# Operand sums and three of the chunk sums on GpSimd instead of VectorE, in a gated scan with two feed-forward layers

## The chip, the core and the metric

The kernel runs on one core of a Trainium2 chip. The metric is device microseconds of one execution. In the profile PE is TensorE's matmuls, PEld its weight loads, DVE is VectorE, ACT is ScalarE, POOL is GpSimd and SP the engine that issues DMAs.

## What is computed

Three stages on 6080 tokens of 256 features, all in float32: a gated scan along the tokens, a feed-forward layer with a leaky ReLU, a second one with an ELU.

```
sig = 1 / (1 + exp(-f_logit));  f = lower_bound + (1 - lower_bound) * sig
h[t] = f[t] * h[t-1] + (1 - f[t]) * x[t]                 # the scan, 256 features
y1 = max(0.01 * a, a) @ w_out1,      a = h  @ w_in1      # 256 -> 2048 -> 256
y2 = elu(b) @ w_out2,                b = y1 @ w_in2      # 256 -> 2048 -> 256
```

## The kernel before

**Tiling.** Tokens go in 12 chunks: 11 of 512 and one of 448 (the fifth). Features lie on the 128 partitions, tokens along the free axis. The 2048 inner features are taken in 4 groups (q = 0 to 3) of 512. For every layer, chunk and group there is an in-projection, the activation, and an out-projection that adds into the chunk's output banks. A chunk of a layer takes PE about 40 us.

**Precision.** Each float32 operand is split in a high part (a cast to fp32r, by ScalarE) and a low part (value less high part, by VectorE), and each product is made of three matmuls (lines 611, 612, 613).

**Seven products instead of eight.** The in-projection of a chunk (from the third chunk of layer 1 on, and in all of layer 2) is done as a 2 x 2 block product with seven block products and some sums (Strassen's way, in Winograd's form). The sums of the weights are made once. The sums of the data are made for each chunk in operands(): four subtractions of 128 x 256, T1 to T4, on the tile bt (the helper comb, line 455). T2 needs T1, T4 needs T2. Then split() casts the blocks to their high parts on ScalarE (L459) and makes their low parts on VectorE (L461), in three pieces: the plain blocks B11, B22, B21; then T1, T2, T3; then T4. The splits are held back until the group before the chunk's first has begun (hold). The tile bt exists once: its next filling, by two scans (L579) in layer 1, by two DMAs from y1d (L599) in layer 2, begins when the last split is done.

**Inside a group** the seven products run into two banks and one seed bank. Products feed each other through snapshots: ScalarE copies a bank (L658, L694), VectorE adds bank and snapshot (L661, one input in PSUM), and the next products go into the banks that these leave free. The activations are L707, L712 (layer 1) and L717 to L734 (layer 2); the gated values are split for the out-projection by L750 and L753.

**Two groups of four** have their odd half of the out-projection done with seven products too (seven(); chunks 4 to 12 of layer 1 with q = 1, 2, and chunks 1 to 11 of layer 2 with q = 0, 1). Their operands are summed in odd_operands() (L842) and split there (L854, L857). They leave two further banks, "s" and "z", which leave() folds into the chunk's two output banks: ScalarE copies both into an SBUF tile of four quarters (L903); u2 (L905) adds quarter 1 to quarter 2; u4 (L906) adds that to quarter 0; L907 adds quarters 0 and 1 to output bank 1; "both" (L910, 128 x 512, its second input one quarter read twice) makes a partial sum in SBUF; L915 adds output bank 0 to it. In layer 1 the result goes to y1d by DMA; in layer 2 it is transposed (L929) and stored.

**Banks.** There are 7 PSUM banks and one seed bank, handed out from a pool in the planned order.

**The order of the work.** Nothing is issued as it stands in the code. Each step is handed to a planner (class Plan, emit) as an operation of an engine with a cost formula (v1, v2 for VectorE, s1 for ScalarE, mm for PE), the operations it comes after, the tiles it takes and gives back, and a due time that is carried backwards through the operations that use it. The planner starts, engine by engine, the operation that can start first, and among those that can start within 0.1 us the one that is due first. The order that comes out is fixed in each engine's queue, and each engine works its queue in order. Before the change GpSimd has one kind of planned operation, sg (L368, in weights()): 32 instructions of one input, 128 x 512, which help to rebuild the weights' float32 values. The last 16 of them are spread over 165 to 406 us.

Of the kernel before, what the change touches and what calls it, by code (L numbers as in the profile page):

```python
# [15 lines left out]
ALU = mybir.AluOpType  # L16
# [96 lines left out]
def kernel(  # L113
# [24 lines left out]
    nc = tc.nc  # L138
# [69 lines left out]
    def v1(n):  # L208
        return 0.07 + n / 960.0
# [3 lines left out]

    def s1(n):
        return 0.09 + n / 1200.0

    def mm(n):
        return (n * 0.000451 + 0.0025 if n < CH else 0.2272) if n != HC else 0.1136
# [6 lines left out]
    def dve(*a, **k):  # L225
        return plan.add("DVE", *a, **k)

    def act(*a, **k):
        return plan.add("ACT", *a, **k)

    def pool(*a, **k):
        return plan.add("POOL", *a, **k)

    def dma(*a, **k):
        return plan.add("SP", *a, **k)

    def free(after, give):

        plan.add("-", 0.0, 1e6, lambda: None, after, give=give)
# [18 lines left out]
    for l, c, q in stream:  # L258
        n = sizes[c]
# [52 lines left out]
    def weights(l, u, due, gate=()):  # L312
# [45 lines left out]
        def val():  # L358
# [10 lines left out]
            out=fr(), in0=top().bitcast(I8), scalar1=2.0, scalar2=-2.0, op0=ALU.min, op1=ALU.max,  # L369
        ), [ld], take=[(b, "wf", "ws")])  # L370
        ex = act(s1(n) + 0.1, None, lambda: nc.scalar.activation(
            out=sc().bitcast(I32), in_=tile_("up"), func=AF.Relu, scale=2.0**27, bias=gbias,
        ), [up, sg], give=[(b, "up", "up")])
# [64 lines left out]
    def operands(c, filled, take, read=(), hold=()):  # L438


        n = sizes[c]
        h = n // 2
        xb = {"done": {}}
        bt = take

        def f32(s, e=None):
            return bt["bt"][2].bitcast(F32)[:, s * h : (e or s + 1) * h]

        def part(j, s, e):

            name, s, e = ("pb", s - 1, e - 1) if 1 <= s < 4 else ("pt", s and s - 3, (s and e - 3) or 1)
            return xb[name][2][:, 4 * HC * j + s * h : 4 * HC * j + e * h]

        def comb(o, i, j, after):
            return dve(v1(h), None, lambda: nc.vector.tensor_tensor(
                out=f32(o), in0=f32(i), in1=f32(j), op=ALU.subtract), after)

        def split(s, e, after, last):
            hi = act(s1((e - s) * h), None, lambda: nc.scalar.copy(out=part(0, s, e), in_=f32(s, e)), after,  # L459
                     take=[(xb, "pb" if s == 1 else "pt", "op")] if s else [])  # L460
            lo = dve(v1((e - s) * h), None, lambda: nc.vector.tensor_tensor(  # L461
                out=part(1, s, e), in0=f32(s, e), in1=part(0, s, e).bitcast(F32), op=ALU.subtract,
            ), [hi], give=[(bt, "bt", bt["pool"])] if last else [])
            for i in range(s, e):
                xb["done"][i] = [lo]
            return hi, lo

        t1 = comb(T1, B12, B11, filled[:1])
        t3 = comb(T3, B22, B12, filled)
        t2 = comb(T2, B22, T1, [t1] + filled[1:])  # L470
        t4 = comb(T4, B21, T2, [t2, t1, t3])
        one = split(1, 4, [*filled, *hold], False)
        two = split(4, 7, [t1, t2, t3, one[0], *hold], False)
        split(0, 1, [t4, two[0], one[1], two[1], *read], True)

        def op(s):
            return tuple(part(j, s, s + 1) for j in (0, 1))

        xb["op"] = op
        return xb  # L480

    def rows(c, filled, take, read=()):
# [26 lines left out]
        out=fa, in0=lb, scalar1=-0.5, scalar2=0.5, op0=ALU.mult, op1=ALU.add), [ab])  # L509
    ab = dve(0.07, None, lambda: nc.vector.tensor_scalar(  # L510
        out=fb, in0=lb, scalar1=0.5, scalar2=0.5, op0=ALU.mult, op1=ALU.add), [ab])
# [353 lines left out]
    def leave(l, c, i, yb, swapped):  # L865
        n, t0 = sizes[c], starts[c]
        if swapped:
            for t in range(n // P):
                ob = {}

                def move(t=t, ob=ob):
                    dst, ps = ob["o"][2][:, :D], yb[t // 2][2][:, t % 2 * D : (t % 2 + 1) * D]
                    if t // 2:
                        nc.vector.tensor_copy(out=dst, in_=ps)
                    else:
                        nc.scalar.copy(out=dst, in_=ps)

                def send(t=t, ob=ob):
                    nc.sync.dma_start(out=out[t0 + t * P : t0 + (t + 1) * P, :], in_=ob["o"][2][:, :D])

                ev = (dve if t // 2 else act)(v1(D), due_in[i] + 20.0, move, [yb["touched"][t // 2]],
                                              take=[(ob, "o", "raw" if t % 2 else "t")],
                                              give=[(yb, t // 2, "bank")] if t % 2 else [])
                dma(DMA, due_in[i] + 20.0, send, [ev], give=[(ob, "o", "raw" if t % 2 else "t")], late=LATE)
            return
        h = n // 2
        soon = due_in[i] + 26.0
        last = yb["touched"]
        ob = {k: {} for k in range(KD)}
        pool_ = "t" if l == 1 else "raw"  # L890

        def o(k):
            return ob[k]["o"][2][:, :n]

        done = {}
        if "s" in last:

            sb = {}

            def at(s, e=None):  # L900
                return sb["sb"][2][:, s * h : (e or s + 1) * h]

            cps = [act(s1(n), soon, lambda s=s, k=k: nc.scalar.copy(out=at(s, s + 2), in_=yb[k][2][:, :n]), [last[k]],  # L903
                       take=[(sb, "sb", "h")] if s == 0 else [], give=[(yb, k, "bank")]) for s, k in ((0, "s"), (2, "z"))]
            u2 = dve(v1(h), soon, lambda: nc.vector.tensor_tensor(out=at(2), in0=at(2), in1=at(1), op=ALU.add), cps)  # L905
            u4 = dve(v1(h), soon, lambda: nc.vector.tensor_tensor(out=at(0), in0=at(0), in1=at(2), op=ALU.add), [u2])  # L906
            done[1] = dve(v1(n), soon, lambda: nc.vector.tensor_tensor(  # L907
                out=o(1), in0=yb[1][2][:, :n], in1=at(0, 2), op=ALU.add), [u4, last[1]],
                take=[(ob[1], "o", pool_)], give=[(yb, 1, "bank")])
            both = dve(v1(n), soon, lambda: nc.vector.tensor_tensor(  # L910
                out=o(0).rearrange("p (a h) -> p a h", a=2),
                in0=at(0, 4).rearrange("p (a b h) -> p a b h", a=2, b=2)[:, :, 0, :],
                in1=at(3).unsqueeze(1).to_broadcast([P, 2, h]), op=ALU.add), [u4], take=[(ob[0], "o", pool_)])
            free([done[1], both], [(sb, "sb", "h")])
            done[0] = dve(v1(n), soon, lambda: nc.vector.tensor_tensor(  # L915
                out=o(0), in0=o(0), in1=yb[0][2][:, :n], op=ALU.add), [both, last[0]], give=[(yb, 0, "bank")])
        elif l == 1:
            for k in range(KD):
                done[k] = (act if k else dve)((s1 if k else v1)(n), None, lambda k=k: (
                    nc.scalar.copy if k else nc.vector.tensor_copy)(out=o(k), in_=yb[k][2][:, :n]),  # L920
                    [last[k]], take=[(ob[k], "o", pool_)], give=[(yb, k, "bank")])
        if l == 1:
            yd[c] = [dma(DMA, due_in[i] + 30.0, lambda k=k: nc.sync.dma_start(
                out=y1d[c][k * P : (k + 1) * P, :], in_=o(k)), [done[k]], give=[(ob[k], "o", pool_)], late=LATE)
                for k in (1, 0)]
            return
        for k in (1, 0):
            tb = {}
            tr = dve(v1(n), None, lambda tb=tb, k=k: nc.vector.transpose(  # L929
                out=tb["o"][2][:, :n], in_=o(k) if done else yb[k][2][:, :n]), [done.get(k), last[k]], take=[(tb, "o", "t")],  # L930
                give=[(ob[k], "o", pool_) if done else (yb, k, "bank")])
            sent = []
            for z in range(4):
                def send(tb=tb, k=k, z=z):
                    c0 = k * P + z * 32
                    nc.sync.dma_start(
                        out=out[t0 : t0 + n, c0 : c0 + 32].rearrange("(b i) j -> i b j", i=32),
                        in_=tb["o"][2][z * 32 : (z + 1) * 32, :n].rearrange("p (b j) -> p b j", j=32),
                    )

                sent.append(dma(DMA, due_in[i] + 40.0, send, [tr] + sent[-1:], give=[(tb, "o", "t")] if z == 3 else [],
                                late=LATE if z == 3 else 0.0))
# [19 lines left out]
    for i, (l, c, q) in enumerate(stream):  # L962
# [18 lines left out]
        at = len(prods)  # L981
# [40 lines left out]
```

## Time and profile before

| | |
|---|---|
| median of 3 runs | 998.78 us (998.7 to 1000.65) |
| span of the profiled execution | 999.4 us, 20315 instructions |
| PE busy | 986.1 us (99%) |
| PEld busy | 974.7 us (98%) |
| VectorE busy | 877.2 us (88%), 1352 instructions |
| ScalarE busy | 773.7 us (77%), 1135 instructions |
| GpSimd busy | 32.1 us (3%), 38 instructions |

The page gives no time of the profiled execution besides its span, the time from the first to the last instruction; the runs shown are executions of their own. A busy share is an average over the whole span. Neighbouring instructions of one engine overlap by some 0.08 us in the records, so that a group's busy time is a little more than the time that its engine spends on it.

### The profile page before, as it was taken

Reading aid. Unit: us, or ns where it says so; the run is one execution under the profiler, and the core shown is the slowest. Engines: PE = TensorE matmul, PEld = TensorE weight load, DVE = VectorE, ACT = ScalarE, POOL = GpSimd, SP = SyncE. Lnnn points to the kernel's source line nnn. Section 1 sums busy time; section 2 is a strip of 40 time slices with the busy share of each in tenths; the row PEclk is TensorE's granted clock in tenths of the full one; section 3 lists DMA queues with packets and bytes.
Section 4 is the critical chain, followed back from the end, with each engine's and each line's share of the span. In section 5 each row is a group of like instructions: output and inputs, shape, how many; then the busy total and the mean of one; then the engine's idle time right before and its main releaser. Section 6 shows DMA issues by size and latency. Waiting matters only on the chain.

```text
span 999.4 us, 20315 instructions
## 1 busy us (share of the span) xinstructions
PE 986.1 (99%) x8338; PEld 974.7 (98%) x8338; DVE 877.2 (88%) x1352; ACT 773.7 (77%) x1135; POOL 32.1 (3%) x38
## 2 busy tenths in 40 slices
PE   7999999999999999999999999999999999999998
PEld 6999999999999999999999999999999999999997
DVE  6899978999999999986678998988989989889875
ACT  5776687878978878777678787877887888788864
POOL 1111000010000000100000000000000000000000
PEclk9999999999999999999999999999999999999999
DMA  6533304155353553411760101101111021010110
GB/s 189 137 96 75 81 11 95 56 146 130 122 158 105 130 135 98 107 33 53 274 253 22 22 22 40 23 22 22 30 34 22 23 44 22 22 23 22 33 22 22
DMA packets 159086, 74.38 MB, mean 74 GB/s; under 512 B 132496, under 2 KB 146832, under 8 KB 158992
## 3 DMA queue, kind: packets, MB, share of 16 engines
q1 hardware_dynamic: 158992, 73.08, 27.1%
q8 instruction: 65, 1.06, 0.4%
q14 instruction: 29, 0.24, 0.1%
HBM read 48.01 MB, written 25.03 MB: 73 GB/s over the span
## 4 chain that ended last, share of the span: by engine, by line
PE 97%; DVE 1%; DMA 1%; ACT 0%; SPq 0%; issue 0%; DVEq 0%
PE bank L611 29%; PE bank L613 29%; PE bank L612 29%; PE seed L613 2%; PE seed L612 2%; PE seed L611 2%; DMA raw<-in_f_logit_dram 1%; PE bank L799 1%; PE bank L797 0%; PE bank L798 0%; DVE op L753 0%; PE bank L543 0%; DVE ws L378 0%; DVE ws L723 0%; DVE bt L579 0%
## 5 line engine op out<-in xcount | busy, mean ns | idle before, releaser
L613 PE MATMUL bank<-op,wI 128*128 128x256 f32 (+1 forms) x1152 | 319.3, 277 | 0.8 <-DVE wI L392 0.8
L611 PE MATMUL bank<-op,wI 128*128 128x256 f32 (+1 forms) x1152 | 320.0, 278 | 0.0
L612 PE MATMUL bank<-op,wI 128*128 128x256 f32 (+1 forms) x1152 | 319.1, 277 | 0.0
L611 PEld LDWEIGHTS bank<-op,wI 128*128 128x128 f32 x1152 | 217.4, 189 | 1.9 <-ACT sn L658 0.2
L612 PEld LDWEIGHTS bank<-op,wI 128*128 128x128 f32 x1152 | 217.3, 189 | 1.5 <-DVE op L498 0.2
L613 PEld LDWEIGHTS bank<-op,wI 128*128 128x128 f32 x1152 | 217.4, 189 | 1.2 <-DVE wI L392 1.2
L611 PE MATMUL bank<-op,wE 128*128 128x256 f32 (+2 forms) x662 | 191.1, 289 | 0.0
L612 PE MATMUL bank<-op,wE 128*128 128x256 f32 (+2 forms) x662 | 191.0, 288 | 0.0
L612 PE MATMUL bank<-op,wO 128*128 128x256 f32 (+2 forms) x680 | 189.4, 279 | 1.5 <-DVE op L753 1.5
L613 PE MATMUL bank<-op,wE 128*128 128x256 f32 (+2 forms) x662 | 190.8, 288 | 0.0
L611 PE MATMUL bank<-op,wO 128*128 128x256 f32 (+2 forms) x680 | 189.4, 278 | 0.0
L613 PE MATMUL bank<-op,wO 128*128 128x256 f32 (+2 forms) x680 | 189.2, 278 | 0.0
L661 DVE TENSOR_TENSOR h<-bank,sn 128x512 f32<-128x512 f32 (+1 forms) x176 | 119.5, 679 | 39.0 <-PE bank L613 30.0
L612 PEld LDWEIGHTS bank<-op,wO 128*128 128x128 f32 x680 | 127.8, 188 | 1.8 <-DVE op L753 1.7
L613 PEld LDWEIGHTS bank<-op,wO 128*128 128x128 f32 x680 | 127.9, 188 | 0.2
L611 PEld LDWEIGHTS bank<-op,wO 128*128 128x128 f32 x680 | 127.8, 188 | 0.1
L613 PEld LDWEIGHTS bank<-op,wE 128*128 128x128 f32 x662 | 124.4, 188 | 2.3
L658 ACT COPY sn<-bank 128x512 f32<-128x512 f32 (+1 forms) x176 | 102.1, 580 | 31.2 <-PE bank L613 29.1
L611 PEld LDWEIGHTS bank<-op,wE 128*128 128x128 f32 x662 | 124.5, 188 | 1.2
L612 PEld LDWEIGHTS bank<-op,wE 128*128 128x128 f32 x662 | 124.4, 188 | 1.0
L753 DVE TENSOR_TENSOR op<-h,op 128x1024 fp32r<-128x1024 f32 (+1 forms) x78 | 94.8, 1215 | 9.1 <-ACT op L750 8.8
L753 DVE TENSOR_TENSOR op<-ws,op 128x1024 fp32r<-128x1024 f32 (+1 forms) x74 | 88.5, 1209 | 15.3 <-ACT op L750 15.3
(109 smaller groups left out, 1819.4 us busy)
## 6 DMA issues: line engine op xcount, KB each, us to landing
ws<-in_moe_w_in_dram SPq DMA_DIRECT2D x32, 255.6 KB, 3.7
ws<-in_moe_w_out_dram SPq DMA_DIRECT2D x32, 255.6 KB, 3.2
w2dI<-ws SPq DMA_DIRECT2D x16, 448.0 KB, 2.8
wI<-w2dI SPq DMA_DIRECT2D x8, 896.0 KB, 6.3
y1d<-t SPq DMA_DIRECT2D x22, 256.0 KB, 2.1
bt<-y1d SPq DMA_DIRECT2D x22, 256.0 KB, 2.9
out_dram<-t SPq DMA_DIRECT2D x80, 64.0 KB, 2.0
raw<-in_f_logit_dram SPq DMA_DIRECT2D x72, 64.0 KB, 2.9
```

The source lines that it names most:

```text
L611: nc.tensor.matmul(ps[:, s], wop[0], a[0][:, s], start=start and z == 0, stop=False, skip_group_check=True)
L612: nc.tensor.matmul(ps[:, s], wop[0], a[1][:, s], start=False, stop=False, skip_group_check=True)
L613: nc.tensor.matmul(ps[:, s], wop[1], a[0][:, s], start=False, stop=stop, skip_group_check=True)
L658: return act(s1(2 * h), None, lambda: nc.scalar.copy(out=ps(name), in_=ps("X")), after, take=[(b, name, "sn")])
L661: return dve(v1(2 * h), None, lambda: nc.vector.tensor_tensor(out=half(name, s), in0=two(ps(bank)), in1=two(ps(sn)), op=ALU.add), after, **k)
L753: gates[name] = dve(v1(2 * n), None, lambda name=name, g=g: nc.vector.tensor_tensor(out=gate(name, 1), in0=whole(g), in1=gate(name, 0).bit ...
L799: nc.tensor.matmul(dst, al, wh, start=False, stop=False, skip_group_check=True)
```

## The change

A cost formula for GpSimd's two-input operations is added, and four kinds of operation are handed to GpSimd instead of VectorE, with that cost: comb in operands() (4 per chunk, 22 chunks), and u2, u4 and "both" in leave() (20 chunk ends). What they compute, on which tiles, and what they come after stays. The other sums (combine, odd_operands, L661, L907, L915) stay on VectorE. As the planner is given other engines and other costs, it orders all engines' queues anew.

```diff
     def s1(n):
         return 0.09 + n / 1200.0
 
+    def p2(n):
+        return 0.1 + n * 0.0022
+
...
         def comb(o, i, j, after):
-            return dve(v1(h), None, lambda: nc.vector.tensor_tensor(
+            return pool(p2(h), None, lambda: nc.gpsimd.tensor_tensor(
                 out=f32(o), in0=f32(i), in1=f32(j), op=ALU.subtract), after)
...
-            u2 = dve(v1(h), soon, lambda: nc.vector.tensor_tensor(out=at(2), in0=at(2), in1=at(1), op=ALU.add), cps)
-            u4 = dve(v1(h), soon, lambda: nc.vector.tensor_tensor(out=at(0), in0=at(0), in1=at(2), op=ALU.add), [u2])
+            u2 = pool(p2(h), soon, lambda: nc.gpsimd.tensor_tensor(out=at(2), in0=at(2), in1=at(1), op=ALU.add), cps)
+            u4 = pool(p2(h), soon, lambda: nc.gpsimd.tensor_tensor(out=at(0), in0=at(0), in1=at(2), op=ALU.add), [u2])
             done[1] = dve(v1(n), soon, lambda: nc.vector.tensor_tensor(
                 out=o(1), in0=yb[1][2][:, :n], in1=at(0, 2), op=ALU.add), [u4, last[1]],
                 take=[(ob[1], "o", pool_)], give=[(yb, 1, "bank")])
-            both = dve(v1(n), soon, lambda: nc.vector.tensor_tensor(
+            both = pool(p2(n), soon, lambda: nc.gpsimd.tensor_tensor(
                 out=o(0).rearrange("p (a h) -> p a h", a=2),
```

## Rows read from the trace of the kernel before

**Rows 1.** The page: busy time by engine (share of span, instructions); chain by engine.

```profile
PE 986.1 (99%) x8338; PEld 974.7 (98%) x8338; DVE 877.2 (88%) x1352; ACT 773.7 (77%) x1135; POOL 32.1 (3%) x38
...
PE 97%; DVE 1%; DMA 1%; ACT 0%; SPq 0%; issue 0%; DVEq 0%
```

**Rows 2.** Windows: length, busy PE, PEld, DVE, ACT, POOL (instructions), clock, DMA share, GB/s.

```profile
225.00:400.00 175.00, 175.00 (x1496) 173.38 (x1494) 170.22 (x276) 146.07 (x221) 9.09 (x11) 1.00 0.45 126
540.00:940.00 400.00, 400.00 (x3409) 396.39 (x3408) 364.98 (x541) 322.99 (x449) 0.00 (x0) 1.00 0.13 28
```

**Rows 3.** Waits (us, times, longest): PE whole span, first and last; PEld 30 to 985.

```profile
PE bank L543 <- DMA raw<-in_f_logit_dram: 3.6, 2, 2.9
...
PE bank L613 <- DVE wI L392: 0.8, 1, 0.8
...
PEld bank L611 <- ACT sn L658: 0.2, 1, 0.2
```

**Rows 4.** Source lines of moved instructions: count, ns min/median/max, first and last start, forms.

```profile
L455 DVE TENSOR_TENSOR bt<-bt x88: 380/417/883, 67.0 to 912.0; 128x256 f32<-128x256 f32 x80, 128x224 f32<-128x224 f32 x8
...
L905 DVE TENSOR_TENSOR h<-h x20: 382/418/426, 190.1 to 947.1; 128x256 f32<-128x256 f32 x18, 128x224 f32<-128x224 f32 x2
...
L910 DVE TENSOR_TENSOR raw<-h x11: 617/683/692, 549.5 to 950.1; 128x512 f32<-128x512 f32 x10, 128x448 f32<-128x448 f32 x1
```

**Rows 5.** Timeline (start, us, engine, line): the turn at 627 to 633, and ACT's split.

```profile
627.21 2.35 DVE L753 TENSOR_TENSOR op<-ws,op 128x1024 fp32r<-128x1024 f32 x2
...
631.42 1.11 DVE L455 TENSOR_TENSOR bt<-bt 128x224 f32<-128x224 f32 x3
632.91 0.69 DVE L661 TENSOR_TENSOR h<-bank,sn 128x512 f32<-128x512 f32 x1 [0.38 <-PE bank L613]
...
658.13 0.77 ACT L459 CAST op<-bt 128x672 fp32r<-128x672 f32 x1
```

**Rows 6.** Source line L368, GpSimd's own instructions.

```profile
L368 POOL TENSOR_SCALAR ws<-ws x32: 643/669/3229, 8.3 to 403.4; 128x512 f32<-128x512 int8 x32
```

**Rows 7.** Timeline, DVE and POOL where both work, layer 1.

```profile
165.50 1.01 DVE L307 TENSOR_TENSOR wO<-h,wO 128x384 fp32r<-128x384 f32 x1
...
203.79 3.23 POOL L368 TENSOR_SCALAR ws<-ws 128x512 f32<-128x512 int8 x1 [21.63 <-DVE h L842]
...
205.10 1.08 DVE L857 TENSOR_TENSOR op<-h,op 128x896 fp32r<-128x896 f32 x1
...
288.66 1.32 DVE L455 TENSOR_TENSOR bt<-bt 128x256 f32<-128x256 f32 x2
...
289.06 0.65 POOL L368 TENSOR_SCALAR ws<-ws 128x512 f32<-128x512 int8 x1 [18.07 <-DVE bt L455]
...
328.35 0.68 DVE L661 TENSOR_TENSOR h<-bank,sn 128x512 f32<-128x512 f32 x1
...
328.45 0.65 POOL L368 TENSOR_SCALAR ws<-ws 128x512 f32<-128x512 int8 x1 [14.41 <-DVE op L753]
...
405.33 1.69 DVE L857 TENSOR_TENSOR op<-h,op 128x1024 fp32r<-128x1024 f32 x1
```

**Rows 8.** Timeline of ACT, DVE and PE in the turn at 228 to 240.

```profile
228.34 0.54 ACT L903 COPY h<-bank 128x448 f32<-128x448 f32 x1
...
235.85 0.60 DVE L915 TENSOR_TENSOR t<-t,bank 128x448 f32<-128x448 f32 x1
236.38 1.04 DVE L571 SCALAR_TENSOR_TENSOR t<-t,t 128x512 f32<-128x512 f32 x1
...
238.66 0.66 DVE L661 TENSOR_TENSOR h<-bank,sn 128x512 f32<-128x512 f32 x1
...
239.19 0.28 PE L613 MATMUL bank<-op,wI 128*128 128x256 f32 x1
239.38 0.38 PE L611 MATMUL bank<-op,wI 128*128 128x256 f32 x1
239.60 0.28 PE L612 MATMUL bank<-op,wI 128*128 128x256 f32 x1
```

## The prediction

> **What bounds the kernel now.** I read the page's busy line and its chain first: PE is busy 986.1 of 999.4 us and is 97% of the chain that ended last [rows 1]. Then the windows: PE fills 175.00 of 175 us in the stretch 225 to 400 and 400.00 of 400 from 540 to 940, at granted clock 1.00, the 2.4 GHz level [rows 2]. The waits say the same: PE's six rows are 9.4 us together, from L543's 3.6 to L392's 0.8, all on lines of the start or the end, and between 30 and 985 us its weight loads wait four times 0.2 us, the matmuls not at all [rows 3]. So this is one PE stream with a head and a tail, and a change gains only where PE waits: under 1 us in that stretch. DVE is the second engine, busy 170.22 of 175 us in the dense stretch, and in the second layer 364.98 of 400, or 36.5 in a chunk of 40 [rows 2]. A busy DVE is no bound by itself; what counts is whether one of its results comes late for PE.
>
> **What the change takes from DVE.** 88 combs (L455), and L905, L906 and L910 20 times each; L906 is like L905, and of L910 the 9 of layer 1 are like the 11 shown [rows 4]. Neighbouring DVE instructions overlap, so I cost a comb by a run of them: three fill 1.11 us, 0.37 each [rows 5], and L905 and L906 the same. L910 is 0.68 us [rows 4]. That is 128 x 0.37 + 20 x 0.68 = 61 us, and in a 40 us chunk that has both kinds 6 x 0.37 + 0.68 = 2.9 us.
>
> **What it adds to GpSimd.** The trace has no two-input GpSimd instruction. The nearest row is L368, one input of 512 columns: 643 ns at least, 669 in the middle, 3229 at most [rows 6]. A comb reads 2 x 256 columns, so I take 0.65 us, the undisturbed L368, to which it is nearest; L910's copy reads 2 x 512, so 1.3 us. Together 128 x 0.65 + 20 x 1.3 = 109 us on an engine that is busy 32.1 us now [rows 1]. The two ends: as cheap as on DVE (61 us), or each as long as the longest L368 (148 x 3.2 = 474 us, under half the span). At neither end is GpSimd the bound.
>
> **What GpSimd's work costs DVE.** Here the rows are plain. An L368 runs from 289.06 to 289.71; the two combs that began at 288.66 take 1.32 us where two take 0.74, and end 0.27 us after it: the second one was held until GpSimd was done [rows 7]. It goes the other way too: the L368 of 203.79 needs 3.23 us, because two-input DVE instructions, the L857 of 205.10 among them, pass ahead of it at their usual length [rows 7]. And L661, with one input in PSUM, isn't held: 0.68 us beside an L368 of 0.65 [rows 7]. I paired the 16 L368 after 160 us with the DVE instructions beside them: 11 lengthened one, by 0.27 to 0.47 us against its usual length, together 4.1 us; the first is L307 at 165.50, the last L857 at 405.33 [rows 7]. Of 16 x 0.65 = 10.4 us of GpSimd time that is a share of 0.40. On 109 us it makes 43 us of new delay, against 61 us taken off: DVE's load falls a little, by 18 us. It breaks even at a share of 0.56. The ends are 0 and the whole 109 us.
>
> The Trainium skill's page "SBUF — State Buffer", section "Who interferes with whom", says that a DVE instruction with two SBUF inputs contends with a GpSimd instruction that reads SBUF, that the second to issue fully blocks until the first is done, and that a DVE instruction with one SBUF input outside the 2-port modes doesn't contend. The held comb and the undisturbed L661 agree; that several DVE instructions in a row passed one waiting L368 is more than it says. Its page "GPSIMD Engine Reference", section "Performance versus the Vector engine", gives 4497 ns for a tensor_tensor of 2048 columns; scaled by columns that is an estimate of 0.56 and 1.12 us, and the delay would be 38 us in place of 43.
>
> **What of it reaches PE.** The 11 delays are a test that the kernel before has already made, most of them in its densest DVE stretch, where PE shows no wait [rows 2, 3]. At one place the matmul pitch opens: matmuls start at 239.19, 239.38 and 239.60, where 0.117 us separates two neighbours of 175 us / 1496 [rows 2, 8]; 0.18 us is lost. The DVE rows ahead of it say why: L571 at 236.38, one of the eleven, took 1.04 us, and so L661 began only at 238.66 and ended 0.06 us before the matmul of 239.38 [rows 8]. So 4.1 us of DVE delay cost PE 0.18 us, one part in 23, and 43 us would cost 1.9 us. Against it stands the relief, which comes in the same place. In the turn of 627 to 633 the seven GpSimd instructions would run beside two L753 of 2.35 us together, two-input instructions that can be held, and L661; but the three combs that now stand right ahead of the L661 of 632.91 are gone, 1.11 us, and this L661 waits 0.38 us for PE already [rows 5]. I halve the 1.9 us: **+1 us**.
>
> **Latency of the moved steps** costs nothing where I look. The combs of that turn are done at 632.5, and ACT's split of them begins at 658.13, 25 us later [rows 5] (shorter in layer 1, where the loads and scans fill the chunk). The chain L905, L906, L910 starts when the copies L903 are done (228.34 + 0.54) and L915 follows at 235.85, 7.0 us later, the shortest such distance of the 20 turns [rows 8]; on GpSimd the chain needs 0.65 + 0.65 + 1.3 = 2.6 us undisturbed. What covers it is the chunk's last out-projection, for which L907 and L915 wait anyway. If that cover is gone (three instructions of 3.23 us are 9.7 us), DVE stands up to 2.7 us at L915 with the next L661 queued behind it, for which PE waits. No DMA is moved. In GpSimd's queue L368 now comes behind up to seven others, 5.2 us; its product is a weight of layer 2, wanted much later.
>
> **Sum.** Head and tail: the moved instructions lie between 67.0 and 951 us [rows 4], so they stay. Stream: +1 us. On the profile's span of 999.4 that is 1000.4; the median of the runs, 998.78, lies 0.6 under that span, so I forecast 999.8 us. Two kernels of this length can't be told apart within about 0.2%, 2 us, so that is **no change**.
>
> **Rivals.**
> 1. *Slower: a held DVE instruction stands ahead of L661.* GpSimd's seven instructions come in one burst a chunk, not singly as L368 does. If DVE pays all 5.2 us of it and gets 2.9 back, it lags 2.3 us. DVE's idle time is 3.5 us a chunk in layer 2, but 4.8 in 175, 1.1 a chunk, in the dense stretch: 4.4 chunks x 1.2 = 5 us lost there. And one L661 in each of 20 turns that comes 0.3 us late (a delay of 0.47 less the 0.17 that it may have to spare) is another 6. By one or both, 1003 to 1011, middle 1006. It decides from a share of 0.56 upwards, or where bursts outrun the spare time at a lower one. The skill's full block, with DVE always second, is this case. For it: two-input instructions are the larger part of DVE's work. Against it: the eleven delays. Chance 0.34.
> 2. *Slower: the chain on GpSimd is late*, kept out as at 203.79, and DVE waits in L907 or L915. Layer 1 has nine such turns; 0.3 to 1 us lost in each, of the 2.7 above, is 3 to 9 us: 1002 to 1008. Chance 0.08.
> 3. *Faster: the relief reaches PE.* Under 1 us in the stream; over 2 us only if the order, planned anew with the new costs, also shortens the tail: 996.5. Chance 0.08.
> 4. *It doesn't do what it says:* the new order leaves DVE as busy and PE as full. Same time as the forecast, and within its chance.
>
> **How the numbers follow.** Forecast 0.50: 998 to 1000.8. Same 0.50, slower 0.34 + 0.08 = 0.42, faster 0.08. The range runs from 997.5, which leaves out most of the faster case, to 1009, which leaves out the upper quarter of the slower ones.
>
> **What would show it.** Right: GpSimd busy 130 to 180 us, L455 near 0.65 us and some at 1 to 3; DVE's two-input groups (L753, L857, L734) 0.05 to 0.2 us longer in the mean, L661 and L723 as before; DVE busy within 25 us of 877; PE full from 30 to 985. Wrong: PE waits for L661 in the stream, or its pitch opens at each turn (rival 1); DVE idle ahead of L907 or L915 for GpSimd (rival 2); shorter waits at the tail (rival 3). A share well above 0.56, read from the lengthened groups, would upset the forecast first.

## The result and the profile after

The kernel after takes 1014.63 us (median of 4, 1012.14 to 1015.78), the one before 999.71 (4 runs, 998.7 to 1001.17): ratio 1.0150, 95% interval 1.0134 to 1.0165. The change costs 15 us; no change had been forecast, and 1014.6 lies above the range. The profiled execution took 1015.78 us, span 1014.0. Lines of the new kernel behind its helper `p2` stand 3 higher than before: L661 is now L664, L753 is L756, L455 is L458. Below, single executions of several kernels, the one before among them, came out some 10 us above their median, and two at granted clocks of 0.755 (the profiled one of chunk_sums_only) and 0.56 (one of old_order_one_column) are left out, so that ratios have wide intervals, and differences under 0.5% are read from the traces.

The page's busy time by engine, and its chain by engine, of the kernel after; beside it stand [rows 1]:

```profile
PE 995.3 (98%) x8338; PEld 980.2 (97%) x8338; DVE 857.0 (85%) x1204; ACT 774.6 (76%) x1135; POOL 191.5 (19%) x186
...
PE 86%; DVE 8%; ACT 3%; issue 2%; DMA 1%; SPq 0%; DVEq 0%; ACTq 0%
```

DVE has become 20 us lighter, much as forecast (18). Yet it now holds 8% of the chain that ended last, and PE has lost 11 points of it. Windows (length; busy PE, PEld, DVE, ACT, POOL with instructions; granted clock; DMA share; GB/s) tell where. Before:

```profile
30.00:160.00 130.00, 129.99 (x1113) 128.63 (x1112) 113.42 (x195) 93.95 (x155) 9.45 (x12) 1.00 0.31 75
160.00:420.00 260.00, 260.00 (x2194) 257.14 (x2192) 248.05 (x405) 214.13 (x325) 17.98 (x16) 1.00 0.45 122
420.00:520.00 100.00, 100.00 (x872) 99.47 (x871) 71.75 (x106) 73.35 (x105) 0.00 (x0) 1.00 0.39 140
520.00:760.00 240.00, 240.00 (x2025) 237.47 (x2025) 218.30 (x328) 192.70 (x270) 0.00 (x0) 1.00 0.13 30
760.00:980.00 220.00, 220.00 (x1904) 218.65 (x1903) 197.38 (x282) 175.19 (x240) 0.00 (x0) 1.00 0.13 26
```

After:

```profile
30.00:160.00 130.00, 128.30 (x1105) 126.71 (x1104) 111.79 (x182) 93.41 (x156) 22.54 (x24) 1.00 0.31 74
160.00:420.00 260.00, 258.81 (x2146) 254.05 (x2146) 239.88 (x361) 208.65 (x318) 58.78 (x58) 1.00 0.46 123
420.00:520.00 100.00, 100.00 (x862) 99.46 (x861) 62.20 (x81) 72.02 (x105) 16.04 (x17) 1.00 0.37 130
520.00:760.00 240.00, 237.36 (x1962) 233.47 (x1961) 208.56 (x277) 188.74 (x265) 45.78 (x42) 1.00 0.14 35
760.00:980.00 220.00, 220.00 (x1908) 218.66 (x1907) 195.78 (x255) 176.59 (x242) 44.01 (x36) 1.00 0.13 25
```

The matmul counts are to be read, more than the busy time: from 160 to 420 us PE is still busy 258.81 of 260, but starts 48 matmuls fewer, 5.7 us of its work at 260 us / 2194 each; from 520 to 760 it is 63 fewer, 7.5 us. (The mix of widths in a window shifts a little, so these are rough.) From 760 on nothing is lost, with as much GpSimd work as in the stretch before. The granted clock is 1.00 throughout.

PE's weight loads from 30 to 985 us waited 0.8 us in all before [rows 3]; after (us, times, longest):

```profile
PEld bank L614 <- ACT sn L661: 3.8, 8, 1.1
PEld bank L614 <- DVE h L664: 2.0, 4, 1.0
PEld bank L616 <- DVE wI L395: 1.8, 2, 1.6
PEld bank L614 <- ACT seed L697: 1.3, 3, 1.0
PEld bank L615 <- DVE op L860: 0.7, 1, 0.7
PEld seed L616 <- DVE wI L395: 0.4, 1, 0.4
```

That is 10.0 us. To separate these waits from slower running, I took all distances between the starts of neighbouring matmuls, up to 14 us before the last. A distance 0.03 us or more above the usual one of its width (0.1133 us for 256 columns) is a **stall**, a smaller excess is **pitch**. Before has 1.6 us of stalls and 6.1 of pitch, after 11.1 and 11.0. So of the 14.6 us by which the two spans differ, stalls are 9.5, pitch 4.9 and the head 0.25. Stalls by stretch, before and after: 0.8 and 2.8 from 30 to 160; 0.4 and 3.8 from 160 to 420; none from 420 to 520; 0.2 and 4.3 from 520 to 760; 0.2 in both after that.

**One stall, followed back.** Before, DVE's timeline (start, us) around 74 us, an operand's step and the steps that unpack a weight:

```profile
73.99 1.22 DVE L753 TENSOR_TENSOR op<-h,op 128x1024 fp32r<-128x1024 f32 x1
75.13 0.69 DVE L378 TENSOR_TENSOR ws<-ws 128x512 f32<-128x512 f32 x1
75.73 0.69 DVE L299 TENSOR_TENSOR h<-wI 128x512 f32<-128x512 f32 x1
76.33 0.87 DVE L365 TENSOR_SCALAR up<-ws 128x512 uint8<-128x512 uint8 x1
77.12 0.68 DVE L392 TENSOR_TENSOR wI<-ws,wI 128x512 fp32r<-128x512 f32 x1
```

After, DVE, GpSimd and PE in the same place:

```profile
74.11 3.92 POOL L458 TENSOR_TENSOR bt<-bt 128x256 f32<-128x256 f32 x3 [2.89 <-DVE bt L582]
...
74.53 1.75 DVE L756 TENSOR_TENSOR op<-h,op 128x1024 fp32r<-128x1024 f32 x1
76.21 1.22 DVE L381 TENSOR_TENSOR ws<-ws 128x512 f32<-128x512 f32 x1
77.35 1.23 DVE L302 TENSOR_TENSOR h<-wI 128x512 f32<-128x512 f32 x1
78.50 0.86 DVE L368 TENSOR_SCALAR up<-ws 128x512 uint8<-128x512 uint8 x1
79.28 0.68 DVE L395 TENSOR_TENSOR wI<-ws,wI 128x512 fp32r<-128x512 f32 x1
...
80.02 0.39 PE L616 MATMUL bank<-op,wI 128*128 128x256 f32 x1 [1.38 <-DVE wI L395]
```

Three combs in a row hold three DVE instructions in a row, each by 0.53 or 0.54 us, and are held themselves: 3.92 us for three. L395, after GpSimd's burst, runs as before. DVE's L368, with one input, takes 0.86 us, twice its usual 0.42, and before (as L365) it took 0.87: in both kernels one of GpSimd's own 32 steps runs beside it. L395 begins 2.2 us later than before, 1.6 of it from the three holds and 0.5 from earlier; that is more than the spare time here, and PE stands. It is the same at 522 us, where four combs hold a chain of short steps:

```profile
522.19 3.38 POOL L458 TENSOR_TENSOR bt<-bt 128x256 f32<-128x256 f32 x4 [2.38 <-DMA bt<-y1d]
...
521.84 0.42 DVE L845 TENSOR_TENSOR h<-ws 128x256 f32<-128x256 f32 x1
522.30 0.92 DVE L845 TENSOR_TENSOR h<-ws,h 128x256 f32<-128x256 f32 x1
523.13 0.96 DVE L845 TENSOR_TENSOR h<-ws 128x256 f32<-128x256 f32 x1
524.01 0.95 DVE L845 TENSOR_TENSOR h<-ws,h 128x256 f32<-128x256 f32 x1
524.89 1.76 DVE L737 SCALAR_TENSOR_TENSOR ws<-ws,h 128x1024 f32<-128x1024 f32 x1
526.57 0.95 DVE L860 TENSOR_TENSOR op<-ws,op 128x768 fp32r<-128x768 f32 x1
...
527.57 0.38 PE L615 MATMUL bank<-op,wO 128*128 128x256 f32 x1 [0.54 <-DVE op L860]
530.50 0.39 PE L614 MATMUL bank<-op,wI 128*128 128x256 f32 x1 [0.78 <-DVE h L664]
```

The first L845 shows the undisturbed length, 0.42; the next three take 0.92 to 0.96. L860 comes late for the matmul of 527.57, and DVE is still behind when it reaches L664, for which the matmul of 530.50 waits.

Half of the waits above, 5.1 of 10.0 us, end on ScalarE's copies L661 and L697. In the three longest of these stalls ScalarE is late because it stood behind DVE. At 555 us:

```profile
552.27 1.29 POOL L913 TENSOR_TENSOR raw<-h 128x512 f32<-128x512 f32 x1
...
552.34 1.77 DVE L732 TENSOR_SCALAR ws<-h 128x1024 f32<-128x1024 f32 x1
...
554.14 1.06 ACT L735 ACTIVATE ws<-ws 128x1024 f32<-128x1024 f32 x1 [1.51 <-DVE ws L732]
...
555.74 0.38 PE L614 MATMUL bank<-op,wI 128*128 128x256 f32 x1 [0.76 <-ACT seed L697]
```

ScalarE waits 1.51 us for L732, so its copy L697 comes late, and PE waits for the copy. At 200 us ScalarE waited 1.37 us for the scan L582, at 723 us 1.17 for L737. L732 has one input and takes 0.69 us in the middle; here it takes 1.77. So an instruction with one input can be held too: of the 79 held ones counted below, some 9 have one input.

### The profile page after: what moved, and what is told of

Same layout as the page of the kernel before. It is cut to its first block, busy times and chain, and to the rows that moved or that the text cites. A ratio compares the mean times of both kernels' runs of the same rounds, so it can differ in the third digit from the quotient of the medians.

```text
span 1014.0 us, 20411 instructions
## 1 busy us (share of the span) xinstructions
PE 995.3 (98%) x8338; PEld 980.2 (97%) x8338; DVE 857.0 (85%) x1204; ACT 774.6 (76%) x1135; POOL 191.5 (19%) x186
## 4 chain that ended last, share of the span: by engine, by line
PE 86%; DVE 8%; ACT 3%; issue 2%; DMA 1%; SPq 0%; DVEq 0%; ACTq 0%
PE bank L614 26%; PE bank L616 26%; PE bank L615 26%; PE seed L616 2%; PE seed L615 2%; PE seed L614 2%; DVE op L756 1%; DVE h L664 1%; DVE bt L582 1%; DVE ws L381 1%; DMA raw<-in_f_logit_dram 1%; PE bank L802 1%; PE bank L800 0%; ACT op L753 0%; PE bank L801 0%
## 5 line engine op out<-in xcount | busy, mean ns | idle before, releaser
L664 DVE TENSOR_TENSOR h<-bank,sn 128x512 f32<-128x512 f32 (+1 forms) x176 | 119.4, 678 | 65.8 <-PE bank L616 47.9
L661 ACT COPY sn<-bank 128x512 f32<-128x512 f32 (+1 forms) x176 | 102.1, 580 | 32.1 <-PE bank L616 30.7
L458 POOL TENSOR_TENSOR bt<-bt 128x256 f32<-128x256 f32 (+1 forms) x88 | 89.5, 1029 | 160.4 <-DVE bt L582 130.1
L756 DVE TENSOR_TENSOR op<-ws,op 128x1024 fp32r<-128x1024 f32 (+1 forms) x74 | 102.3, 1395 | 18.5 <-ACT op L753 18.0
```

The costliest lines, as they stand in the source:

```text
L458: return pool(p2(h), None, lambda: nc.gpsimd.tensor_tensor(out=f32(o), in0=f32(i), in1=f32(j), op=ALU.subtract), after)
L661: return act(s1(2 * h), None, lambda: nc.scalar.copy(out=ps(name), in_=ps("X")), after, take=[(b, name, "sn")])
L664: return dve(v1(2 * h), None, lambda: nc.vector.tensor_tensor(out=half(name, s), in0=two(ps(bank)), in1=two(ps(sn)), op=ALU.add), after, **k)
L756: gates[name] = dve(v1(2 * n), None, lambda name=name, g=g: nc.vector.tensor_tensor(out=gate(name, 1), in0=whole(g), in1=gate(name, 0).bit ...
```

## The experiments

In the table, *held* counts DVE instructions more than 0.06 us longer than usual for their form, and the sum of that excess. Stalls and pitch are as above.

| kernel | ratio to before (95%) | stalls, us | pitch, us | held, us |
|---|---|---|---|---|
| before | | 1.6 | 6.1 | 19, 7.2 |
| after | 1.0150 (1.0134 to 1.0165) | 11.1 | 11.0 | 79, 40.7 |
| one_column | 1.0041 (0.9994 to 1.0088) | 1.0 | 9.2 | 19, 7.1 |
| write_only | 1.0038 (0.9999 to 1.0077) | 2.1 | 14.9 | 19, 6.5 |
| combs_only | 1.0138 (1.0062 to 1.0214) | 13.2 | 11.1 | 73, 31.9 |
| chunk sums alone | 1.0106 (1.0028 to 1.0183) | 8.9 | 13.8 | 48, 27.0 |
| old_order | 1.0094 (1.0064 to 1.0125) | 5.1 | 10.2 | 80, 41.8 |
| old_order_one_column | 1.0016 (0.9980 to 1.0051) | 1.2 | 9.3 | 18, 5.8 |
| new_order_vector | 1.0172 (1.0129 to 1.0214) | 14.9 | 10.5 | 16, 5.8 |
| one_comb | 1.0035 (1.0005 to 1.0065) | 2.1 | 8.5 | 33, 11.7 |
| reserved | 1.0158 (1.0119 to 1.0196) | 10.2 | 11.1 | 87, 39.4 |
| price_2x | 1.0113 (1.0097 to 1.0129) | 10.2 | 9.3 | 84, 38.7 |
| before_512_all | 1.0035 (1.0012 to 1.0058) | 2.0 | 9.0 | 18, 6.2 |

**Is it what GpSimd reads, or the new order?** In one_column every moved sum stays in place, in the order of after, but on one column of its operands; the other columns are left out (shown for comb, the chunk sums likewise):

```diff
-                out=f32(o), in0=f32(i), in1=f32(j), op=ALU.subtract), after)
+                out=f32(o)[:, :1], in0=f32(i)[:, :1], in1=f32(j)[:, :1], op=ALU.subtract), after)
```

> The changed kernel with every moved sum shrunk to its first column (the other columns of T1 to T4 and of the chunk sums are left out); order and queues stay those of the changed kernel, and GpSimd clears the tile bt once at the start, when it is idle. Theory 1 (GpSimd's reads hold two-input DVE instructions, in bursts, and PE pays): GpSimd's time on SBUF is almost gone, so 998 to 1001 us, DVE's L756 back at 1.21 us. Theory 2 (the newly planned order is worse in itself): still 1011 to 1016. Theory 3 (the moved sums come too late for those who wait): 998 to 1001, as in theory 1.

Its profiled span was 1000.2. The added stalls are gone, and with them the added holds. PE's weight loads wait once:

```profile
PEld bank L614 <- ACT sn L661: 0.2, 1, 0.2
```

So the order of after, by itself, stalls nothing. This rests on the trace and not on the time: the ten executions took 1002.0 to 1014.5 us, median 1008.0, outside the expected 998 to 1001, and the profiled one was the fastest; what the others lost is open. In write_only GpSimd's time stays, but is spent on writing, one column of the sum and then three memsets of the others:

```diff
+        def wr(out_, in0, in1, op):
+            nc.gpsimd.tensor_tensor(out=out_[:, :1], in0=in0[:, :1], in1=in1[:, :1], op=op)
+            for _ in range(3):
+                nc.gpsimd.memset(out_[:, 1:], 0.5)
```

> The changed kernel with every moved sum replaced by a one-column sum and three fills of the other columns with a constant (the sums themselves are left out): GpSimd stays busy about as long per step, but reads almost nothing. Theory 1 (reads hold DVE): 998 to 1002 us. A variant of it in which GpSimd's writes hold DVE as well: 1008 to 1016. Theory 2 (order): 1011 to 1016. Theory 3 (late results): 1008 to 1016, since the steps take as long as before.

The page's busy line, then a group by line (busy us, mean ns; idle before it):

```profile
PE 994.1 (99%) x8338; PEld 982.8 (98%) x8338; DVE 825.7 (82%) x1204; ACT 774.6 (77%) x1135; POOL 221.9 (22%) x630
```

```profile
L760 DVE TENSOR_TENSOR op<-ws,op 128x1024 fp32r<-128x1024 f32 (+1 forms) x74 | 88.7, 1212 | 20.5 <-ACT op L757 20.5
```

The same group of after (its L756 is L760 here):

```profile
L756 DVE TENSOR_TENSOR op<-ws,op 128x1024 fp32r<-128x1024 f32 (+1 forms) x74 | 102.3, 1395 | 18.5 <-ACT op L753 18.0
```

GpSimd is busier than in after, 221.9 us against 191.5, and adds next to no holds (19 in all, as many as before): 1212 ns, where after has 1395. Two L368, with one input, grew by 0.23 us each beside a sum's one column and its fills. What holds DVE is, in the main, that GpSimd reads. (The profiled execution, 1009.4 us, has 2.1 us of stalls and 14.9 of pitch; the median, 1004.2, lies above the expected 998 to 1002.) The Trainium skill, "SBUF — State Buffer", section "Who interferes with whom", says that a GpSimd instruction that only writes doesn't contend with a two-input DVE instruction; this run agrees.

**Which of the two parts?** In combs_only the three sums of a chunk's banks go back to DVE, in chunk_sums_only the combs do. The edit of chunk_sums_only, against after:

```diff
-            return pool(p2(h), None, lambda: nc.gpsimd.tensor_tensor(
+            return dve(v1(h), None, lambda: nc.vector.tensor_tensor(
```

> Only the four operand sums of a chunk on GpSimd, the three chunk sums back on VectorE. Theory 1: the four combs are the longer burst (88 instructions, 90 us of GpSimd time of the 162 that were added), so they carry more than half: 1006 to 1011 us. Theory 3 (late results): the combs have some 25 us before they are read, so 999 to 1001.

> Only u2, u4 and both on GpSimd, the operand sums back on VectorE. Theory 1: 60 instructions, 72 us of GpSimd time, in bursts of three: 1003 to 1008 us. Theory 3 (late results): these have the shortest distance to their reader, so most of the 15 us: 1009 to 1015.

> The kernel with only the three chunk sums on GpSimd once more, for its profile. If stalls go with the held DVE time: 60 of the 148 instructions, 25 to 35 instructions held for 12 to 18 us, stalls of the stream 3 to 6 us.

The ratio of chunk_sums_only comes from three executions; chunk_sums_look is the same kernel run again (1014.89 us), and gives the stalls. Each part costs nearly the whole: 13.2 us of stalls for the combs, 8.9 for the sums, 11.1 for both, and medians of 1016.8 and 1014.0 us, each above what had been expected (48 instructions held for 27.0 us, not 25 to 35 for 12 to 18). The costs don't add; each of the kernels is planned anew, so their orders differ too.

**The old order with GpSimd, the new order with DVE.** old_order is the kernel before with the four operations on GpSimd, but still planned, priced and placed as DVE's; new_order_vector is the kernel after, its four operations on DVE at the places planned for GpSimd. The edit of old_order, against before (u2, u4 and both likewise):

```diff
-            return dve(v1(h), None, lambda: nc.vector.tensor_tensor(
+            return dve(v1(h), None, lambda: nc.gpsimd.tensor_tensor(
```

> The kernel before, planned with VectorE's costs and queues as before, but the 148 moved sums issued by GpSimd: every other queue keeps the order of the kernel before. Theory 1 (GpSimd's reads hold two-input DVE instructions in bursts, and PE stands): GpSimd takes a sum as soon as its data are there, so the bursts come in the same places as in the changed kernel, and the stalls of the matmul stream are 8 to 14 us as there (11.1): 1008 to 1016 us. Theory 2 (the new order is worse): 998 to 1002.

> The changed kernel's planned order of all queues, but the 148 sums issued by VectorE, at the places where the plan started them on GpSimd. Theory 1: no GpSimd reads beside L368, DVE gets back 55 us of work that the plan did not foresee: stalls of the stream 1 to 6 us, 1000 to 1006. Theory 2 (the order): stalls near 11 us, 1010 to 1016.

DVE is held as long in the old order as in the new (41.8 and 40.7 us), and PE stalls half as long, 5.1 against 11.1, which neither theory had. And DVE with its own work back in the new order, 61 us that its plan doesn't hold, does no less harm with no hold added (14.9). The longest group of weight-load waits in each, first old_order, then new_order_vector:

```profile
PEld bank L611 <- DVE h L661: 2.6, 5, 1.1
```

```profile
PEld bank L614 <- DVE h L664: 8.1, 12, 1.6
```

So PE stalls when DVE is late against its plan, whether it was held or given more. How much of the 11.1 us is due to the order isn't separated by this: with the holds the old order has half, and without them the new one has none (one_column). That led to the theory that the plan fails by giving the freed time of DVE away.

**Does reserving DVE's time help?** reserved plans each moved sum's old time on DVE as an empty step, right ahead of the sum (shown for comb); price_2x gives GpSimd's sums a price near what they took (1.05 us for 256 columns, where after's plan has 0.66):

```diff
+            hold_ = dve(v1(h), None, lambda: None, after)
             return pool(p2(h), None, lambda: nc.gpsimd.tensor_tensor(
-                out=f32(o), in0=f32(i), in1=f32(j), op=ALU.subtract), after)
+                out=f32(o), in0=f32(i), in1=f32(j), op=ALU.subtract), [*after, hold_])
```

```diff
-        return 0.1 + n * 0.0022
+        return 0.1 + n * 0.0037
```

> The changed kernel, but the plan also sets aside on VectorE, ahead of each moved sum, the time that VectorE would need for it (no instruction is issued there). Theory: the stalls come from DVE delays that the plan does not know of, because it has given away the 55 us that DVE was relieved of. Then the instructions held stay as many (about 79, 41 us), and the stalls of the stream fall from 11.1 to 1 to 5 us: 1003 to 1009 us. Rival: held instructions cost the same whatever the plan knows: stalls 8 to 13 us, 1010 to 1016.

> The changed kernel with GpSimd's cost in the plan at 0.1 + 0.0037 per column (1.05 us for 256 columns, about what the trace of the changed kernel shows, 1.04), VectorE's costs as they were. If the plan's fault is that it takes GpSimd for too fast and the results come late: stalls fall below 4 us, 1000 to 1006. If it is that DVE is held: stalls 8 to 13 us, 1010 to 1016.

Both keep 10.2 us of stalls. That theory fell. What halves them in the old order isn't reserved time nor the price; it stays open.

**What the relief is worth, and what a few holds cost.** old_order_one_column is old_order with the sums on one column; one_comb is the kernel before with one comb in four (22 of 88) on GpSimd:

```diff
+            if o == T3:
+                return pool(p2(h), None, lambda: nc.gpsimd.tensor_tensor(
+                    out=f32(o), in0=f32(i), in1=f32(j), op=ALU.subtract), after)
```

> The kernel before in its own order, with the 148 sums issued by GpSimd and shrunk to one column (the other columns left out; tile bt cleared once at the start): VectorE is relieved of 55 us at no price. What this gains is the most that the move could bring in that order. Expected from PE's waits (under 1 us in the stream): stalls below 1.6 us, 997 to 1001 us. If the relief is worth something to PE: below 996.

> The kernel before with one of a chunk's four operand sums, T3, on GpSimd (22 instructions, never two in a row). If the stalls come from delays that add up in a burst: below 1.5 us of stalls beyond those of the kernel before, as the 11 single delays beside L368 cost 0.2 us; 999 to 1003. If they go with the amount of GpSimd work: a quarter of those of the four combs (13.2 us), 3 to 4 us, 1002 to 1006.

With all 61 us gone from DVE and no more held than before, PE's stalls fall from 1.6 to 1.2 us, and in one_column to 1.0: the relief is worth 0.4 to 0.6 us, since PE had few waits to lose. With 22 combs that come singly, 4.5 us more are held and stalls grow by 0.5, one part in 9. (The time of one_comb, 1004.2 us, lies in the range of the other theory; 2.4 us of it are added pitch.)

**Pitch.** Part of the loss is no stall. In old_order_one_column PE's starts around 377.4 us:

```profile
377.30 0.28 PE L613 MATMUL bank<-op,wO 128*128 128x256 f32 x1
377.41 0.32 PE L611 MATMUL bank<-op,wI 128*128 128x256 f32 x1
377.56 0.28 PE L612 MATMUL bank<-op,wI 128*128 128x256 f32 x1
377.68 0.28 PE L613 MATMUL bank<-op,wI 128*128 128x256 f32 x1
```

Up to 377.41 they come every 0.11 us; a weight load then came late by 0.04 us, and from there they come every 0.12 (0.1133 and 0.1178 in the unrounded records), for tens of us. The window 380 to 405 of this kernel and, in the second fence, of the kernel before:

```profile
380.00:405.00 25.00, 25.00 (x214) 25.00 (x213) 23.16 (x34) 20.80 (x33) 4.73 (x9) 1.00 0.43 129
```

```profile
380.00:405.00 25.00, 25.00 (x223) 25.00 (x223) 24.90 (x42) 21.44 (x33) 2.32 (x2) 1.00 0.39 122
```

PE is busy 25.00 of 25 at granted clock 1.00 in both, and starts 214 matmuls in one, 223 in the other. (The mix of widths may differ a little.) Of the 256-column matmuls about 11% run at the slower pitch before, 25% after. A 512-column block seemed at times to end such a stretch, so before_512_all gives all four groups of a chunk of the kernel before such a block, where only the first has one (504 matmuls of 512 columns, not 126); before_again, before_again2 and after_again are the two kernels unchanged, to see whether the pitch belongs to the program or to the execution:

```diff
-        unbroken = (r, j) == ("E", 1) and q < 1
+        unbroken = (r, j) == ("E", 1)
```

> The kernel before, with the last even block of every group's out-projection in 512-column matmuls, not only in a chunk's first group. The traces show the 256-column matmuls at two pitches, 0.1133 and 0.1178 us; the slow one begins at a small stall and often ends at a 512-column block, which comes once a chunk. If the block is what ends it, four blocks a chunk make slow stretches short: the share of 256-column matmuls at the slow pitch falls from 0.11 to 0.05 or less, the runs lie closer together, 995 to 999 us. If not: share 0.1 to 0.4 as in the others, 999 to 1004.

> The kernel before once more, unchanged. Of the 14.6 us between the two profiles 9.5 are stalls of the stream and 4.9 stretches in which 256-column matmuls follow each other at 0.1178 us instead of 0.1133. If those stretches belong to the program (they start at a wait that its order contains): pitch loss 5 to 7.5 us as in the first profile (6.1), stalls 1 to 2.5. If they are drawn anew in each execution: pitch loss anywhere from 3 to 15.

> The kernel before a third time, as before_again: pitch loss 5 to 7.5 us if it belongs to the program, else 3 to 15.

> The changed kernel once more, unchanged. Stalls 9 to 13 us (first profile 11.1) if the held instructions fall in the same places each time; pitch loss 10 to 12 us if it belongs to the program (first profile 11.0), else 3 to 15.

In before_512_all 14% of the 256-column matmuls run at the slower pitch, not 5% or less, and the kernel became slower: that theory fell too. (Its pitch loss is 9.0 us; 2.2 of the 2.9 us more lie on the added 512-column matmuls, which take a little over twice the time of one of 256.) The unchanged kernels gave 5.7 and 5.4, and 11.2 (1000.31, 999.0 and 1014.63 us; stalls 1.6, 1.8 and 11.4). So in these five executions the pitch loss goes with the program. That it does so in every execution isn't shown: write_only's profiled one, with 14.9 us, ran at the slower pitch for some 300 us on end, and others of that kernel took 1001.8 to 1012.3 us. As one_column (9.2) and old_order_one_column (9.3) have no more held than before, some 3 of the 4.9 us may come with a changed program alone; what sets them is open.

## Why the prediction was wrong

- **What bounds it, and the relief** held. PE's stream is the bound, and a lighter DVE gives it 0.4 to 0.6 us of stalls (old_order_one_column, one_column).
- **DVE's load** held: 20 us lighter, forecast 18. The moved instructions were 67.7 us of durations, and the others grew by 34 us in sum, forecast 43. L753's group with `ws` grew most, from a mean of 1.209 us to 1.395, 0.19 more, at the upper end of what had been named; L661 stayed at 0.68 [rows 7].
- **GpSimd's prices** were low. A 256-column sum takes 0.73 us at least, not 0.65 (the 0.669 below is one of 224 columns); one of 512 took the 1.3 that was reckoned wherever it ran undisturbed. But many are held by DVE in their turn. Source lines (count; ns min, median, max):

```profile
L458 POOL TENSOR_TENSOR bt<-bt x88: 669/749/1797, 65.0 to 927.1; 128x256 f32<-128x256 f32 x80, 128x224 f32<-128x224 f32 x8
...
L913 POOL TENSOR_TENSOR raw<-h x11: 1162/2154/2273, 552.3 to 961.1; 128x512 f32<-128x512 f32 x10, 128x448 f32<-128x448 f32 x1
```

  GpSimd is busy 191.5 us, not 130 to 180. It isn't the bound, and its results aren't late: no wait of DVE or ScalarE ends on GpSimd, and none of the weight-load waits shown; the step on **latency** held, and rival 2 didn't come.
- **What of it reaches PE** is the step that failed. "One part in 23" came from eleven delays of 0.27 to 0.47 us, each by itself, with spare time around it [rows 7, 8]. It was also read too low: the trace of before has a second opening of 0.19 us, at 281.10. L906 is one of the eleven; from there DVE doesn't pause, and its L661 ends 0.05 us before that matmul:

```profile
270.46 0.81 DVE L906 TENSOR_TENSOR h<-h 128x256 f32<-128x256 f32 x1
...
280.38 0.67 DVE L661 TENSOR_TENSOR h<-bank,sn 128x512 f32<-128x512 f32 x1
...
281.10 0.39 PE L611 MATMUL bank<-op,wI 128*128 128x256 f32 x1
```

  With all 0.4 us of stalls from 160 to 420 us it is one part in 10, and 43 us would have cost some 4 us, still less than half of what came. The 33.5 us of new holds cost 9.5 us of stalls, one part in 3.5. Delay isn't passed on in proportion: a single hold is nearly absorbed (one part in 9 in one_comb), while three or four in a row add up to 2 us before DVE can catch up. That the work comes in bursts stood in the text of rival 1, and not in the sum.
- **Halving for the relief** was wrong with it. The relief gave 0.4 to 0.6 us where nothing was added, and no empty step kept it (reserved); that it is spread over the chunk by the new order, while the hold falls where the burst is, was argued and not shown. Only from 760 us on does the forecast describe what happened: 44.01 us of GpSimd time, 16 DVE instructions held by 9.5 us, and no matmul lost. In combs_only 3.5 us of stalls lie there, so that is no rule of the stretch.
- **Rival 1** is what came, on the condition that it named: the share that was held was 33.5 of the 109 us that the prediction had reckoned for GpSimd, 0.31 (of the 159 us measured 0.21), below 0.56 and below its own 0.40, but bursts outran the spare time. It had 5 us for the dense stretch of layer 1 and 6 for the turns, 11 in all; stalls grew by 3.4 from 160 to 420 us, by 4.1 from 520 to 760 and by 2.0 from 30 to 160, 9.5 in all. That the two sums are so near is partly luck: it had expected 0.3 us in each of 20 turns, and 4.2 of the 4.3 us from 520 to 760 lie at three places (526 to 531, 554 to 556, 723 to 726), with none from 760 on. Its time of 1006 was still too low, and the range with it: no case had a term for the pitch, 4.9 us, which was in the trace of before (6.1 us) behind a PE that is busy 175.00 of 175 [rows 2].

## What to carry to other kernels

Moving work off an engine that isn't the bound gains nothing where the bound has no waits left, and costs what the work does to its neighbours: here GpSimd's reads of SBUF stretched DVE's instructions, most of them with two inputs, by about 0.5 us each time. A trial of single delays doesn't price bursts: add up the holds that follow one another and compare them with the spare time before the next result that the bounding engine waits for. A busy share of 99 or 100% doesn't show an engine at its pace; count its instructions in a window too.

## What the runs showed of the hardware that was not expected

Matmuls of 256 columns follow each other at two steady pitches, 0.1133 and 0.1178 us, at the same granted clock of 1.00. In the place shown the slower one began where a weight load came 0.04 us late; it lasts tens of us, in write_only some 300 on end (100 us of it cost about 4). The loss was nearly the same in the three profiled executions of before (5.4 to 6.1 us) and the two of after (11.0 and 11.2); its cause was not found. GpSimd and DVE, where both read, hold each other in turn: a comb of 256 columns took from 0.727 to 1.797 us, and DVE's L732, with one input, 1.77 us for 0.69.
